# A fused LayerNorm and MLP kernel: another order of loads, statistics and transposes in its opening

## Chip, cores and metric

The kernel runs on one core of a Trainium2 chip. The metric is the device time of one execution in microseconds (us), taken as the median of several runs. All times inside a trace are us from the first instruction of the execution.

## What is computed

x is 2048 x 1024, w1 is 1024 x 3584, w2 is 3584 x 1024, all bfloat16. Cut to what matters:

```python
y = (x - mean(x)) / sqrt(var(x) + 1e-5)          # over the 1024 columns
h = gelu_tanh(y @ w1 + b1)                       # 2048 x 3584
out = h @ w2 + b2                                # 2048 x 1024
```

## The kernel before

The 2048 rows are 16 tiles of 128 rows, and four tiles are one block of 512 rows. For each block the kernel computes all 28 rows of h (a "row" is 128 of the 3584 columns of h, for the 512 rows of x of the block) and then all output chunks of the block. Both products run over the block: 224 matmuls of 128x512 for the first, 224 for the second. Every engine's program is written out as a list of operations with named events. An engine works through its list strictly in that order; an operation that waits holds up everything behind it on its engine.

For blocks 1 to 3 the normalised x is transposed by VectorE while TensorE is busy with the block ahead. Block 0 has nothing ahead of it, so its opening is written out apart, and the change is in that opening alone:

- **Loads.** SP issues x0a (the left half of tile 0), x2, b1, the four pieces w0 to w3 of w1, x3, w4 and then the rest; ScalarE (ACT) issues x0b (the right half of tile 0), x1a and x1b. (Lists at lines 26 and 27; the issue itself is line 182.) w0 and w1 are the upper and lower half of the contraction for rows 0 and 1 of h, w2 and w3 the same for rows 2 and 3. w4 is for rows 4 to 7.
- **LayerNorm on VectorE (DVE).** For each tile there are two bn_stats over 512 columns (line 253), one bn_aggr (line 260), a power on GpSimd (POOL) that makes the inverse deviation (line 257), and the normalisation (line 264). ln_seq (line 278) fixes the order: first statistics of tile i, then the normalisation of tile i-1, then second statistics of tile i, then the aggregate of tile i. So the normalisation of tile 2 stands behind the first statistics of tile 3.
- **Transposes on TensorE (PE).** pe_T (line 316) transposes a tile in eight 128x128 pieces through the identity (line 327); ACT copies the result out of PSUM in two copies of 512 columns (line 333). b1 is transposed in the same way (line 429) and copied to float32 (line 431).
- **First wave.** Before a whole block is there, PE computes rows 0 to 3 of h one tile at a time, with matmuls of 128x128 (line 354): 32 for each tile t, 16 for the upper half of the contraction and 16 for the lower. The eight transposes of tile t+1 (named T1, T2, T3 below) stand between these halves. After the wave come the 128x512 matmuls of rows 4 to 27.
- **Warm-up.** Ahead of the wave PE works through dummy matmuls (line 419): 26 without a gate, 8 behind the first statistics, 8 behind the aggregate, 6 behind the inverse deviation of tile 0, and 3 more after the transposes of tile 0. Line 21 holds these numbers.

The loop of the wave, and the order of the LayerNorm:

```python
for t in range(TPB):
    for h, (j0, j1) in enumerate(KGROUPS):
        for r in range(R):
            pe_cell(0, r, t, t + 1, ..., dts=range(j0, j1))
        if t + 1 < TPB and h == 0:
            pe_T(t + 1)
...
for h in range(2):
    seq.append(op_stats(i, h))
    if h == 0 and prev is not None:
        seq += ops_norm(prev)
seq.append(op_aggr(i))
```

A planner at the end (lines 481 to 496) orders the later work of DVE from estimated times; T_PE_START at line 29 is one of its constants.

Of the kernel before, what the change touches and what calls it, by code (L numbers as in the profile page):

```python
# [5 lines left out]
ACT = mybir.ActivationFunctionType  # L6
ALU = mybir.AluOpType
BF16 = mybir.dt.bfloat16
F32 = mybir.dt.float32
# [10 lines left out]
TAIL_PIECES = 4  # L20
WARM_A = ((26, None), (8, "st0_0"), (8, "mv0"), (6, "rstd0"))
N_WARM_B = 3
W1_CHUNK_COLS = (256, 256, 512, 512, 1024, 1024)
W1_KSPLIT_CHUNKS = 2
N_W2_CHUNKS = 4
SP_FIRST_LOADS = ("x0a", "x2", "b1", "w0", "w1", "w2", "w3", "x3", "w4")
ACT_FIRST_LOADS = ("x0b", "x1a", "x1b")

T_PE_START = 8.5
T_DVE_START = 13.0  # L30
# [54 lines left out]
def bass_standalone__mixer_channel_mlp__prompt_kernel(  # L85
# [20 lines left out]
    assert HC <= 512 and DT * P * 2 <= 2048 and FT >= 4 and FT <= P  # L106
    R = max(1, min(R_WAVE, FT - 2, NB1 - 1))
    nkg = max(1, min(K_GROUPS, DT))
    KGROUPS = [(h * DT // nkg, (h + 1) * DT // nkg) for h in range(nkg)]
    assert NB1 + NB2 + 1 <= 8  # L110

# [30 lines left out]
    with ExitStack() as es:  # L142
# [14 lines left out]
        nhalf = sb("nhalf", [P, NT], F32)  # L157
        st_sb = sb("st_sb", [P, NT, 15], F32)
        mv_sb = sb("mv_sb", [P, NT, 2], F32)
# [4 lines left out]
        ps_2 = ps("ps_2", [P, NB2, 512], F32)  # L164
        ps_1b = ps_1[:, :, :].bitcast(BF16)
        ps_2b = ps_2[:, :, :].bitcast(BF16)
# [38 lines left out]
        def issue(item):  # L205
            if item[0] == "x" and item[-1] in "ab":
                i, h = int(item[1:-1]), "ab".index(item[-1])
                dma(x_sb[:, i, h * HC:(h + 1) * HC], xf[i * P:(i + 1) * P, h * HC:(h + 1) * HC], f"x{i}_{h}",
                    P * HC * 2)
                x_ev[i] = (f"x{i}_0", f"x{i}_1")  # L210
            elif item == "b1":
                dma(b1r_sb[:, :], b1.rearrange("(t p) -> t p", p=P), "b1", F * 2)
            elif item[0] == "x":
                load_x_tile(int(item[1:]))
            elif item[0] == "w" and int(item[1:]) < len(w1_chunks):
                load_w1(int(item[1:]))
# [7 lines left out]
        for i in range(TPB):  # L224
            if i not in x_ev:
                load_x_tile(i)
            else:
                for h, evn in enumerate(x_ev[i]):
                    if evn not in est:
                        issue(f"x{i}" + "ab"[h])  # L230
        if "b1" not in est:
# [16 lines left out]
        pool.op(lambda e: e.memset(nhalf[:, :], -0.5), sig="nhalf")  # L248
        pool.op(lambda e: e.memset(st_sb[:, :, 12:14], 0.0))
        pool.op(lambda e: e.memset(st_sb[:, :, 14:15], LN_EPS * D), sig="eps")  # L250

        def op_stats(i, h):
            return (lambda e, i=i, h=h: e.bn_stats(st_sb[:, i, 6 * h:6 * (h + 1)], x_sb[:, i, h * HC:(h + 1) * HC]),  # L253
                    [x_ev[i][h]], f"st{i}_{h}", 0.65)

        def op_aggr(i):
            pool.op(lambda e, i=i: e.tensor_tensor(out=rstd_sb[:, i:i + 1], in0=mv_sb[:, i, 1:2],  # L257
                                                   in1=nhalf[:, i:i + 1], op=ALU.pow),
                    waits=[f"mv{i}", "nhalf"], sig=f"rstd{i}")
            return (lambda e, i=i: e.bn_aggr(mv_sb[:, i, :], st_sb[:, i, :]),  # L260
                    [f"st{i}_0", f"st{i}_1", "eps"], f"mv{i}", 0.33)

# [8 lines left out]
        def ops_norm(i):  # L271
            if i == 0:
                y_ev[i] = [f"y{i}_{h}" for h in range(2)]
                return [op_norm(i, h * HC, (h + 1) * HC, f"y{i}_{h}") for h in range(2)]
            y_ev[i] = [f"y{i}"] * 2
            return [op_norm(i, 0, D, f"y{i}")]

        def ln_seq(tiles):
            seq = []
            prev = None  # L280
            for i in tiles:
                for h in range(2):
                    seq.append(op_stats(i, h))
                    if h == 0 and prev is not None:
                        seq += ops_norm(prev)
                seq.append(op_aggr(i))
                prev = i
            seq += ops_norm(prev)
            return seq
# [4 lines left out]
        def ops_T(i):  # L294
            blk, t = divmod(i, TPB)
            waits = list(y_ev[i])
            if blk - 2 in mm1_done:
# [15 lines left out]
        pe_t = [T_PE_START]  # L313
        last_te = [None]

        def pe_T(i):
            blk, t = divmod(i, TPB)
            evs = []
            for h, (j0, j1) in enumerate(KGROUPS):
                own = i == 0 and h == 1  # L320
                bank = ps_2b[:, 0, :] if own else ps_t[:, 0, :]
                o0 = j0 if own else 0
                waits = [y_ev[i][h], "ident"]
                if h == 0 and last_te[0] is not None:
                    waits.append(last_te[0])
                for j in range(j0, j1):
                    pe.op(lambda e, i=i, j=j, bank=bank, o0=o0: e.transpose(  # L327
                        out=bank[:, (j - o0) * P:(j - o0 + 1) * P], in_=x_sb[:, i, j * P:(j + 1) * P],
                        identity=ident[:, :]),
                        waits=waits if j == j0 else (), sig=(f"tp{i}_{h}" if j == j1 - 1 else None))  # L330
                src = bank[:, (j0 - o0) * P:(j1 - o0) * P].rearrange("p (j s) -> p j s", j=j1 - j0)
                dst = yT_sb[:, blk % 2, j0:j1, t * P:(t + 1) * P]
                act.op(lambda e, dst=dst, src=src: e.copy(out=dst, in_=src),  # L333
                       waits=[f"tp{i}_{h}" if i == 0 else f"tp{i}_{len(KGROUPS) - 1}"], sig=f"te{i}_{h}")
                evs += [f"te{i}_{h}"] * (j1 - j0)
            yT_ev[i] = evs
            last_te[0] = evs[-1]

        unit_n = [0]
        unit_gelu = []  # L340

        def new_unit():
            u = unit_n[0]
            unit_n[0] += 1
            return u % NB1, ([unit_gelu[u - NB1]] if u >= NB1 else ["b1c"])

        def pe_cell(b, r, t0, t1, bank, waits, sig, dts=None):
# [3 lines left out]
            for k, dt in enumerate(dts):  # L351
                w = (waits if k == 0 else []) + [f"w1c{w1_chunk_of(r, dt)}"]
                w += [yT_ev[b * TPB + t][dt] for t in range(t0, t1)]
                pe.op(lambda e, b=b, r=r, dt=dt, n0=n0, n1=n1, bank=bank: e.matmul(  # L354
                    ps_1[:, bank, n0:n1], lhsT=w1_sb[:, dt, r * P:(r + 1) * P], rhs=yT_sb[:, b % 2, dt, n0:n1],
                    start=(dt == 0), stop=(dt == DT - 1)),
# [5 lines left out]
        def act_gelu(r, t0, t1, bank, wait_ev, sig):  # L362
            n0, n1 = t0 * P, t1 * P
            act.op(lambda e, r=r, n0=n0, n1=n1, bank=bank: e.activation(  # L364
                out=hT_sb[:, r, n0:n1], in_=ps_1[:, bank, n0:n1], func=ACT.Gelu_apprx_tanh,
                bias=b1_sb[:, r:r + 1], scale=1.0),
                waits=[wait_ev, "b1c"], sig=sig)
            unit_gelu.append(sig)

# [16 lines left out]
        def out_chunk(b, st, c0, c1, region, prev_store):  # L386
# [7 lines left out]
            if g >= NB2:  # L394
                waits.append(grp_oe[g - NB2])
            for ft in range(FT):
                pe.op(lambda e, st=st, ft=ft, c0=c0, c1=c1, bank=bank: e.matmul(  # L397
# [19 lines left out]
        def warm(n, gate=None):  # L417
            for _ in range(n):
                pe.op(lambda e: e.matmul(ps_2[:, NB2 - 1, 0:P], lhsT=ones[:, :], rhs=ones[:, :],  # L419
                                         start=True, stop=True), waits=["ones"] + ([gate] if gate else []))  # L420
# [4 lines left out]
        for o in ln_seq(list(range(TPB))):  # L425
            dve_put(o)

        pe_T(0)
        pe.op(lambda e: e.transpose(out=ps_1b[:, NB1 - 1, 0:FT], in_=b1r_sb[:, :], identity=ident[0:FT, 0:FT]),
              waits=["ident", "b1"], sig="b1t")  # L430
        act.op(lambda e: e.copy(out=b1_sb[:, :], in_=ps_1b[:, NB1 - 1, 0:FT]), waits=["b1t"], sig="b1c")  # L431
        warm(N_WARM_B)
        wave = [new_unit() for _ in range(R)]
        for t in range(TPB):
            lastt = (t == TPB - 1)
            for h, (j0, j1) in enumerate(KGROUPS):
                for r in range(R):
                    sig = f"m1_0_{r}" if lastt else f"m1_0_{r}_w{t}"
                    pe_cell(0, r, t, t + 1, wave[r][0], wave[r][1] if (t == 0 and h == 0) else [], sig,
                            dts=range(j0, j1))  # L440
                    if lastt and j1 == DT:
                        act_gelu(r, 0, TPB, wave[r][0], sig, f"g_0_{r}")
                        hT_row[(0, r)] = f"g_0_{r}"
                if t + 1 < TPB and h == 0:
                    pe_T(t + 1)
                    pe_t[0] += DT * 0.056

# [92 lines left out]
```

## Time and profile before

| What | us |
|---|---|
| median of 3 runs | 399.91 |
| lowest and highest of them | 399.84, 399.95 |
| span of the profiled execution, first to last instruction | 398.3 |
| what the median has beyond that span | 1.6 |
| PE busy in the span | 394.9 |
| DVE busy | 137.3 |
| ACT busy | 82.3 |
| first real matmul of the wave starts at | 7.69 |
| last real matmul ends about | 396.5 |

No separate time of the profiled execution is given besides its span; with the 1.6 us around it, it stands at the median. The profile names each group by its source line, engine, operation and tile. "PEld" is the weight load that goes ahead of a matmul. A bracket in a timeline row tells how long the engine had been idle before the row, and what ended the idleness.

### The profile page before, as it was taken

To read this page: it belongs to the slowest core of one execution; us is meant where nothing else is said; L and a number is where in the kernel's file an instruction comes from. 1 tells how busy PE (TensorE), PEld (TensorE's weight loads), DVE (VectorE), ACT (ScalarE), POOL (GpSimd) and SP (SyncE) were. 2 spreads that over 40 slices of the span, in tenths; PEclk is the share of its full clock that TensorE was granted. 3 is DMA by queue.
4 is the path that set the end of the run, shared out by engine and by line. 5 is a ranking of instruction groups with operands and counts; after the bars stand their busy time and mean duration, and the time that the engine had idled before them with its cause. 6 is when DMAs were issued, how large, how long until landed. Compare 5 with 4: busy or idle time off the path is not lost.

```text
span 398.3 us, 4699 instructions
## 1 busy us (share of the span) xinstructions
PE 394.9 (99%) x2056; PEld 189.4 (48%) x2056; DVE 137.3 (34%) x292; ACT 82.3 (21%) x122; POOL 9.7 (2%) x25
## 2 busy tenths in 40 slices
PE   8999999999999999999999999999999999999998
PEld 7744444444444444444444444444444444444447
DVE  5207999899892004988100000001100000001011
ACT  3544430000044332000024334100003344400000
POOL 2002000200010000000000000000000000000000
DMA  8999930000000000000000000000000000000001
GB/s 255 369 387 386 385 146 15 26 13 29 26 1 2 0 0 2 26 15 26 27 15 0 0 2 0 1 27 26 13 28 13 2 0 0 2 13 26 15 26 28
DMA packets 17614, 23.64 MB, mean 59 GB/s; under 512 B 1466, under 2 KB 10042, under 8 KB 17594
## 3 DMA queue, kind: packets, MB, share of 16 engines
q1 hardware_dynamic: 17162, 22.95, 16.6%
q10 hardware_dynamic: 432, 0.39, 0.3%
q8 instruction: 16, 0.26, 0.3%
q14 instruction: 4, 0.03, 0.0%
HBM read 19.14 MB, written 4.19 MB: 59 GB/s over the span
## 4 chain that ended last, share of the span: by engine, by line
PE 99%; ACT 0%; issue 0%; DVE 0%; POOL 0%; POOLq 0%
PE ps L354 49%; PE ps L397 49%; PE ps L419 1%; PE ps_t L327 0%; ACT yT_sb L333 0%; DVE o_sb L408 0%; POOL ones L244 0%; ACT b_sb L431 0%; POOLq L525 0%
## 5 line engine op out<-in xcount | busy, mean ns | idle before, releaser
L354 PE MATMUL ps<-yT_sb,w_sb 128*128 128x512 bf16 (+1 forms) x992 | 194.8, 358 | 0.5 <-ACT b_sb L431 0.5
L397 PE MATMUL ps<-w_sb,hT_sb 128*128 128x512 bf16 (+1 forms) x980 | 194.2, 361 | 0.0
L354 PEld LDWEIGHTS ps<-yT_sb,w_sb 128*128 128x128 bf16 x992 | 91.7, 98 | 102.4 <-ACT b_sb L431 0.7
L397 PEld LDWEIGHTS ps<-w_sb,hT_sb 128*128 128x128 bf16 x980 | 91.3, 98 | 102.6
L364 ACT ACTIVATE hT_sb<-ps,b_sb 128x512 bf16<-128x512 f32 x112 | 76.7, 688 | 257.2 <-PE ps L354 257.2
L305 DVE STREAM_TRANSPOSE yT_sb<-x_sb 32x256 bf16<-32x256 bf16 x192 | 83.7, 436 | 35.0 <-PE ps L354 32.1
L408 DVE TENSOR_TENSOR o_sb<-ps,b_sb 128x512 bf16<-128x512 f32 (+1 forms) x35 | 22.6, 645 | 197.9 <-PE ps L397 197.8
L253 DVE BATCH_NORM_STATS2 st_sb<-x_sb 128x6 f32<-128x512 bf16 x32 | 21.1, 671 | 21.4 <-DMA x_sb<-in_x_dram 21.2
L257 POOL TENSOR_TENSOR rstd_sb<-mv_sb,nhalf 128x1 f32<-128x1 f32 x16 | 8.8, 551 | 111.5 <-DVE mv_sb L260 111.5
L264 DVE TENSOR_SCALAR x_sb<-x_sb,mv_sb,rstd_sb 128x1024 bf16<-128x1024 bf16 (+1 forms) x17 | 8.9, 528 | 3.7 <-POOL rstd_sb L257 2.7
L419 PE MATMUL ps<-ones 128*128 128x128 bf16 x51 | 5.4, 290 | 1.0 <-POOL ones L244 1.0
L419 PEld LDWEIGHTS ps<-ones 128*128 128x128 bf16 x51 | 4.6, 135 | 1.5 <-POOL ones L244 1.0
L333 ACT COPY yT_sb<-ps_t 128x512 bf16<-128x512 bf16 x7 | 3.8, 589 | 7.0 <-PE ps_t L327 7.0
L260 DVE BATCH_NORM_AGGREGATE mv_sb<-st_sb 128x2 f32<-128x15 f32 x16 | 3.6, 222 | 1.5
L327 PE MATMUL ps_t<-ident,x_sb 128*128 128x128 bf16 x28 | 2.2, 220 | 0.0
L422 ACT ACT_TABLE_LOAD x1 | 1.3, 1283 | 2.2 <-issue 2.2
L327 PEld LDWEIGHTS ps_t<-ident,x_sb 128*128 128x128 bf16 x28 | 1.7, 98 | 0.1
L333 ACT COPY yT_sb<-ps 128x512 bf16<-128x512 bf16 x1 | 0.6, 591 | 0.0
L327 PE MATMUL ps<-ident,x_sb 128*128 128x128 bf16 x4 | 0.4, 222 | 0.0
L245 POOL TENSOR_SCALAR_AFFINE_SELECT ident<-ones 128x128 bf16<-128x128 bf16 x1 | 0.3, 294 | 0.1
L327 PEld LDWEIGHTS ps<-ident,x_sb 128*128 128x128 bf16 x4 | 0.2, 98 | 0.1
L244 POOL MEMSET ones<- 128x128 bf16 x1 | 0.2, 205 | 0.3 <-POOLq L525 0.3
(10 smaller groups left out, 1.2 us busy)
## 6 DMA issues: line engine op xcount, KB each, us to landing
w_sb<-in_w_dram SPq DMA_DIRECT2D x4, 1792.0 KB, 18.5
w_sb<-in_w_dram SPq DMA_DIRECT2D x2, 2048.0 KB, 16.7
out_dram<-o_sb SPq DMA_DIRECT2D x31, 128.0 KB, 1.7
x_sb<-in_x_dram SPq DMA_DIRECT2D x3, 1024.0 KB, 14.2
w_sb<-in_w_dram SPq DMA_DIRECT2D x2, 1024.0 KB, 9.2
w_sb<-in_w_dram SPq DMA_DIRECT2D x4, 256.0 KB, 4.7
x_sb<-in_x_dram SPq DMA_DIRECT2D x2, 256.0 KB, 4.4
x_sb<-in_x_dram ACTq DMA_DIRECT2D x3, 128.0 KB, 3.7
```

The lines of the kernel that those rows point to most:

```text
L253: return (lambda e, i=i, h=h: e.bn_stats(st_sb[:, i, 6 * h:6 * (h + 1)], x_sb[:, i, h * HC:(h + 1) * HC]), [x_ev[i][h]], f"st{i}_{h}", 0.65)
L257: pool.op(lambda e, i=i: e.tensor_tensor(out=rstd_sb[:, i:i + 1], in0=mv_sb[:, i, 1:2], in1=nhalf[:, i:i + 1], op=ALU.pow), waits=[f"mv{i} ...
L260: return (lambda e, i=i: e.bn_aggr(mv_sb[:, i, :], st_sb[:, i, :]), [f"st{i}_0", f"st{i}_1", "eps"], f"mv{i}", 0.33)
L264: return (lambda e, i=i, c0=c0, c1=c1: e.tensor_scalar(out=x_sb[:, i, c0:c1], in0=x_sb[:, i, c0:c1], scalar1=mv_sb[:, i, 0:1], scalar2=rst ...
L305: res.append((lambda e, src=src, dst=dst: e.transpose(out=dst, in_=src), waits, (f"tr{i}" if lastop else None), 0.47))
L327: pe.op(lambda e, i=i, j=j, bank=bank, o0=o0: e.transpose(out=bank[:, (j - o0) * P:(j - o0 + 1) * P], in_=x_sb[:, i, j * P:(j + 1) * P], i ...
L333: act.op(lambda e, dst=dst, src=src: e.copy(out=dst, in_=src), waits=[f"tp{i}_{h}" if i == 0 else f"tp{i}_{len(KGROUPS) - 1}"], sig=f"te{i ...
L354: pe.op(lambda e, b=b, r=r, dt=dt, n0=n0, n1=n1, bank=bank: e.matmul(ps_1[:, bank, n0:n1], lhsT=w1_sb[:, dt, r * P:(r + 1) * P], rhs=yT_sb ...
L364: act.op(lambda e, r=r, n0=n0, n1=n1, bank=bank: e.activation(out=hT_sb[:, r, n0:n1], in_=ps_1[:, bank, n0:n1], func=ACT.Gelu_apprx_tanh, ...
L397: pe.op(lambda e, st=st, ft=ft, c0=c0, c1=c1, bank=bank: e.matmul(ps_2[:, bank, 0:c1 - c0], lhsT=hT_sb[:, ft, st * P:(st + 1) * P], rhs=w2 ...
L408: crit.append((est[sig], (lambda e, ob=ob, c0=c0, c1=c1, bank=bank: e.tensor_tensor(out=o_sb[:, ob, c0:c1], in0=ps_2[:, bank, 0:c1 - c0], ...
L419: pe.op(lambda e: e.matmul(ps_2[:, NB2 - 1, 0:P], lhsT=ones[:, :], rhs=ones[:, :], start=True, stop=True), waits=["ones"] + ([gate] if gat ...
```

## The change

The opening of block 0 is arranged anew; the rest of the kernel is as it was.

- **Loads.** Tile 0 comes in four column quarters of 256 columns. SP issues x0a, x0c, x1a, x2, w0 to w3, x3, w4; ACT issues x0b, x0d, x1b, b1.
- **Statistics.** Tile 0 has four bn_stats of 256 columns, and bn_aggr reads 27 values instead of 15. Each tile has its own statistics tensor, so POOL clears them with 32 small memsets instead of 2.
- **Normalisation.** Tile 0 in pieces of 256 and 768 columns, tile 1 in two of 512, tiles 2 and 3 whole as before.
- **Transposes.** Tile 0 in groups of 2, 3 and 3, each with its own PSUM bank and its own copy on ACT; tiles 1 to 3 in two groups of 4, each with its own bank.
- **Order on PE.** For tile 0 rows 0 and 1 are done with both halves of the contraction before rows 2 and 3, piece by piece of the contraction. T1, T2 and T3 stand 8, 16 and 12 matmuls ahead of the end of the part before them (16 in all three before). b1 is transposed behind the matmuls of tile 0, in the bank of the transposes, and the first matmuls wait for b1 no more.
- **Warm-up.** 24 without a gate, 8 behind the first statistics, 8 behind the third, 6 behind the aggregate, 4 behind the inverse deviation, and 4 after the first group of transposes.
- **PSUM.** The first seven accumulation units use the five banks of the first product and the two of the second in turn; then the five go round as before.

```diff
-WARM_A = ((26, None), (8, "st0_0"), (8, "mv0"), (6, "rstd0"))
-N_WARM_B = 3
+WARM_A = ((24, None), (8, "st0_0"), (8, "st0_2"), (6, "mv0"), (4, "rstd0"))
+N_WARM_B = 4
+T_AHEAD = {1: 8, 2: 16, 3: 12}
+NORM_0 = (0, 2, 8)
+GROUPS_0 = (0, 2, 5, 8)
+NORM_1 = {1: (0, 4, 8)}
+GROUPS_1 = (0, 4, 8)
-SP_FIRST_LOADS = ("x0a", "x2", "b1", "w0", "w1", "w2", "w3", "x3", "w4")
-ACT_FIRST_LOADS = ("x0b", "x1a", "x1b")
-
-T_PE_START = 8.5
+X0_PARTS = 4
+SP_FIRST_LOADS = ("x0a", "x0c", "x1a", "x2", "w0", "w1", "w2", "w3", "x3", "w4")
+ACT_FIRST_LOADS = ("x0b", "x0d", "x1b", "b1")
+
+T_PE_START = 6.9
...
-        pool.op(lambda e: e.memset(st_sb[:, :, 12:14], 0.0))
-        pool.op(lambda e: e.memset(st_sb[:, :, 14:15], LN_EPS * D), sig="eps")
+        for i in range(NT):
+            n = 6 * parts(i)
+            pool.op(lambda e, i=i, n=n: e.memset(st_sb[i][:, n:n + 2], 0.0))
+            pool.op(lambda e, i=i, n=n: e.memset(st_sb[i][:, n + 2:n + 3], LN_EPS * D), sig=f"eps{i}")
...
-            return u % NB1, ([unit_gelu[u - NB1]] if u >= NB1 else ["b1c"])
+            bank = first_ring[u] if u < len(first_ring) else ("1", (u - len(first_ring)) % NB1)
+            waits = [bank_gelu[bank]] if bank in bank_gelu else []
...
+        def pe_b1():
+            pe.op(lambda e: e.transpose(out=ps_t[:, 0, 0:FT], in_=b1r_sb[:, :], identity=ident[0:FT, 0:FT]),
+                  waits=["ident", "b1", bank_read["t"]], sig="b1t")
+            act.op(lambda e: e.copy(out=b1_sb[:, :], in_=ps_t[:, 0, 0:FT]), waits=["b1t"], sig="b1c")
+            bank_read["t"] = "b1c"
+
+        pe_T(0, GROUPS_0, 0)
         warm(N_WARM_B)
+        for k in range(1, len(GROUPS_0) - 1):
+            pe_T(0, GROUPS_0, k)
...
+            if t == 0:
+                part = []
+                for r0 in range(0, R, 2):
+                    for j0, j1 in KGROUPS:
+                        part += cells(0, range(r0, min(R, r0 + 2)), j0, j1, True)
+            else:
+                part = []
+                for j0, j1 in KGROUPS:
+                    part += cells(t, range(R), j0, j1, False)
+            if t + 1 < TPB:
+                at = len(part) - T_AHEAD[t + 1]
+                part[at:at] = [("T", t + 1)]
+                if t == 0:
+                    part.append(("b1",))
```

## The prediction

> **What bounds the kernel now.** I read the page first. PE is busy 99% of the span, and the chain that ended last lies on PE for 99%. So the end moves only if PE's continuous work starts earlier or gets a hole. Then I read the chain in order of time:
>
> ```profile
> 1.04 5.04 PE ps L419 x48
> 6.09 0.36 PE ps_t L327 x4
> ...
> 6.47 1.07 ACT yT_sb L333 x2
> 7.54 0.10 ACT b_sb L431
> ...
> 7.69 1.07 PE ps L354 x16
> 8.75 0.45 PE ps_t L327 x8
> 9.20 1.79 PE ps L354 x32
> 10.99 0.47 PE ps_t L327 x8
> 11.46 1.79 PE ps L354 x32
> 13.24 0.45 PE ps_t L327 x8
> 13.69 44.12 PE ps L354 x240
> ```
>
> Columns: start, us, what. From 7.69 on PE never pauses. One 128x128 matmul takes 1.79 / 32 = 0.056 us, one transpose the same (0.45 / 8). From 13.69 on nothing in the change touches PE's work. The question is when the wave can get through, that is, what each piece of it waits for besides PE. The timeline of DVE in the middle of the wave:
>
> ```profile
> 8.37 0.69 DVE L253 BATCH_NORM_STATS2 st_sb<-x_sb 128x6 f32<-128x512 bf16 x1
> 9.15 0.22 DVE L260 BATCH_NORM_AGGREGATE mv_sb<-st_sb 128x2 f32<-128x15 f32 x1
> 9.63 0.69 DVE L253 BATCH_NORM_STATS2 st_sb<-x_sb 128x6 f32<-128x512 bf16 x1 [0.26 <-DMA x_sb<-in_x_dram]
> 10.24 0.53 DVE L264 TENSOR_SCALAR x_sb<-x_sb,mv_sb,rstd_sb 128x1024 bf16<-128x1024 bf16 x1
> ```
>
> The row at 9.63 is the first statistics of tile 3: DVE idles 0.26 until x3 has landed. Behind it stands the normalisation of tile 2, which ends at 10.24 + 0.53 = 10.78. T2's first weight load is the row at 10.83:
>
> ```profile
> 8.54 0.49 PEld L327 LDWEIGHTS ps_t<-ident,x_sb 128*128 128x128 bf16 x8
> ...
> 10.83 0.45 PEld L327 LDWEIGHTS ps_t<-ident,x_sb 128*128 128x128 bf16 x8
> ```
>
> PE arrives there at about the same moment, so the table of waits shows no wait. But there is hardly any reserve: **T2 cannot start before x3 has landed plus about 1.22** (0.61 from the start of the statistics to that of the normalisation, 0.53, 0.05 to PE, 0.02 to wake DVE). Last, the DMA view around two issues, at 3.1 to 3.3 and at 4.2 to 4.4:
>
> ```profile
> w_sb<-in_w_dram SPq DMA_DIRECT2D x2, 256.0 KB, 4.7
> ```
> ```profile
> x_sb<-in_x_dram SPq DMA_DIRECT2D x1, 256.0 KB, 5.3
> ```
>
> The second, issued at 4.28, is x3: it lands 5.3 later, at 9.6, after a queue of everything ahead. The first holds two pieces of w1. The later one, issued at 3.19, is w2, which lands 4.9 after its issue, at 8.0; w3 (issued at 3.74, 5.1) lands at 8.9. From 4 to 9.6 the stretches show 300 to 375 GB/s and a DMA share about 1.0 or above: the queue is full.
>
> **The change, part by part.**
>
> *Loads up to x3.* Ahead of and with x3 stand the same bytes as before: x0 to x3, 1 MB, and w0 to w3, 1 MB, and b1. Only the packets of x0 shrink, from 1 KB to 512 B. Rows: from 5 to 6 there are 665 packets and 0.33 MB (512 B each) at 330 GB/s; from 7 to 8, 544 packets, 298 GB/s; from 9.62 to 11, 478 packets, 0.49 MB (1 KB each), 355 GB/s. x0's 0.262 MB take 0.74 at the last rate and 0.79 to 0.88 at the first two: +0.05 to +0.14, I take +0.1. Upwards: the opening from 1.75 to 3 runs at 131 to 316 GB/s; at 209, its second lowest stretch, x0 takes 1.25 against 0.74, +0.5. Downwards: 0.29 MB have moved by 3.0; at 330 GB/s from 1.8 it would be 0.40, so quarters that fill the opening better could save at most 0.11 / 0.33 = 0.3. SP issues eight DMAs ahead of x3 instead of seven, at about 0.5 each; x3 is issued at 4.8 instead of 4.28 and still waits some 4.9 in the queue, so this costs nothing; without that cover it would cost 0.5. b1 leaves SP's queue for the end of ACT's; the table load on ACT behind it starts 0.45 later (2.18 to 2.6) and ends by 3.9, long before ACT's first copy. So w2 lands at 8.14, w3 at 9.0, x3 at 9.7.
>
> The Trainium skill, "DMA: Bandwidth & Descriptors", section "Bandwidth", speaks against the quarters: its table has 138 GB/s for a DMA of 64 KB, and calls smaller ones descriptor-dominated. An estimate from that rate for x0 is 1.9 us, which would put the time at about 401.1. The trace's rate for DMAs queued behind each other decides here.
>
> *Statistics of tile 0.* DVE starts when x0a has landed: 3.23 before; a quarter brings half the bytes, so between 2.7 (0.13 MB less on both queues at about 250 GB/s) and 3.23. Two statistics of 512 take 1.29 (the row at 3.23: x2); four of 256 take between 1.29 (cost by columns) and 2.5 (cost by instruction: four pitches of 0.61). The normalisations have 0.53 for 1024 columns and about 0.40 for 512, so there is a fixed part; I take 1.45. The aggregate starts between 4.2 and 5.8 and likeliest at 4.4, against 4.61. DVE's next work shifts by as much, and x1a should be there (it is now ahead of x2).
>
> The Trainium skill, "VectorE: DVE Perf Modes", section "The TRN2 errata — SBUF-src ops pay a fixed extra latency per instruction", tells one to keep tiles at 512 elements or more, since each instruction pays the latency again; its 58 cycles at 0.96 GHz give, as an estimate, 2 x 0.06 more for four instead of two, which is 0.1 and moves nothing at T2.
>
> *POOL.* 32 memsets instead of 2. Rows: the two start 0.04 and 0.06 after the operation before them, and last 0.13. At 0.05 apart they end at 1.34 + 1.6 = 2.9, hidden under the wait for x0; at 0.13 one after the other they end at 5.5, and the inverse deviation would come up to 0.9 late. I take the pitch.
>
> *Warm-up and first matmul.* 40 dummies stand ahead of the aggregate's gate; the 26 ungated loads take 2.69 from 1.04, 0.104 each, so 40 end at about 5.3, and ten at 0.056 end at 5.9. Normalisation of 256 columns is ready at about 5.6, so PE gets to the first transposes at 5.9. Two transposes, four dummies, six transposes: 6.6. The copy on ACT (0.59 for 512 columns, 0.4 for 256 by the same kind of scaling) ends at 6.6. The first real matmul is at about **6.65 instead of 7.69**, and it no longer waits for b1.
>
> *What is late next.* Rows 0 and 1 need w0 and w1 (landed 6.3 and 7.2), then the copies; they are through at about 7.8. Rows 2 and 3 need **w2, at 8.14**: PE stands 0.35 there. 8 matmuls to 8.64; T1, 8 transposes, to 9.09 (tile 1 normalised by about 8.3); 8 matmuls to 9.53; the transpose of b1 waits for the first copy of T1 (copy 9.06 to 9.65), 9.76 with it; 16 matmuls of tile 1 to 10.65. Queued behind b1's transpose is all of PE, but this wait is in front of the next one. **T2 needs tile 2 normalised: x3 at 9.71 + 1.22 = 10.93.** PE stands again, 0.28. Behind T2 both kernels have the same work: 16 matmuls of tile 1, tiles 2 and 3, T3. T3 moves 4 matmuls back, which gives its normalisation (ready at 12.92 + 0.1, PE there at 13.4) more room. The copies of T3 have 12 matmuls, 0.67, in front of their first reader and need 0.17 + 0.22 + 0.04 + 0.59 + 0.05 = 1.07 from the start of T3; with its own 0.45 PE gives 1.12. It just fits.
>
> *Later blocks.* PE has no idle time there; the planner's new constant moves a few DVE operations, the transposes for blocks 1 to 3 are long ready. Nothing.
>
> **Sum.** T2 goes from 10.83 to 10.93: span 398.3 + 0.1, with 1.6 around it **400.0**. The gain of 1.0 at the first matmul is eaten by w2 (down to about 0.2 at T2's place) and by x3 (gone).
>
> **Rivals.** What a measurement of this kernel can tell from no change is about 0.2%, 0.8 us.
>
> 1. *The opening moves as a whole* (1.0 earlier: 398.9). It needs w2 and x3 to land 0.8 or more sooner. Against it: a full queue and the same bytes. 0.04.
> 2. *Part of it arrives* : x3 lands as before or up to 0.3 sooner, T2 between 10.5 and 10.83 (PE's side and DVE's free time at about 9.2 allow no earlier): 399.55 to 399.85. 0.15.
> 3. *DVE or POOL late* : statistics by instruction or memsets end to end, +0.7 to +0.9 at the aggregate. DVE's 0.26 of idleness ahead of x3's statistics, and 0.1 for the later x3, are the cover; what exceeds them is paid: 400.25 to 400.6. Also x3 late by 0.5: 400.4. 0.11.
> 4. *PE falls back to the slow pitch* in the wave (the slower side). Place: the stalls at 6.9, 7.8, 9.6 and 10.65, together about 1.1 between 6.65 and 10.93. Price: the slow stretch before lasted 4.3 (1.04 to 5.3) at 0.104 against 0.056; again 4.3 at that pitch loses 2.0: 402.0. It decides from a pause longer than the 0.54 that PE has before 7.69 now, after which the pitch stays 0.056. No single stall of mine is longer. 0.05.
>
> My forecast, T2 held by x3, 399.85 to 400.25: 0.65. The range goes from rival 2's lower end to 400.6: rivals 1 and 4 stay out. Faster by over 0.2%: 0.04; within: 0.90; slower: 0.06.
>
> **What would show it.** Right: first matmul of the wave at 6.5 to 6.8; a wait of PE for w2; x3's statistics again right after a DMA wait, at 9.6 to 9.9; T2 at 10.8 to 11.1 after PE idleness. Wrong: T2 before 10.5 (x3 is not the limit), 0.1 us pitches after 7, or aggregates after 4.9.

## The result

| Kernel | runs | median us | lowest to highest |
|---|---|---|---|
| before | 22 | 399.90 | 399.64 to 400.62 |
| changed | 22 | 400.54 | 400.00 to 401.33 |

The ratio is 1.0013, with a 95% interval of 1.0007 to 1.0019: 0.5 us slower, clear of noise but within the 0.2% that I called no change. (The two medians stand 0.64 apart.) The time lies in the range, 0.54 above the forecast of 400.0, but only 0.06 below the range's upper end: it is in the band of rival 3, and not in the 399.85 to 400.25 to which I gave 0.65. The profiled execution took 400.68, with a span of 399.3, 1.0 above the span before. That difference is on the large side: 398.3 belongs to a short execution of the kernel before, whose spans beside the experiments have medians of 398.5 to 398.7, and the changed kernel's 22 spans have one of 399.05. One execution among the experiments, the profiled one of e1, took 462.69 where its ten neighbours took 399.86 to 401.09, and is left out of e1's ratio.

### The profile page after: what moved, and what is told of

Read it like the earlier page. It is cut to its first block, busy times and chain, and to the rows that moved or that the text cites. A ratio compares the mean times of both kernels' runs of the same rounds, so it can differ in the third digit from the quotient of the medians.

```text
span 399.3 us, 4691 instructions
## 1 busy us (share of the span) xinstructions
PE 393.3 (99%) x2024; PEld 189.4 (47%) x2059; DVE 138.0 (35%) x295; ACT 82.4 (21%) x123; POOL 10.6 (3%) x55
## 4 chain that ended last, share of the span: by engine, by line
PE 97%; DMA 1%; SPq 1%; issue 1%; DVE 0%
PE ps L420 48%; PE ps L375 48%; DMA w_sb<-in_w_dram 1%; SPq L189 1%; PE ps_t L342 0%; PE ps L342 0%; DVE o_sb L431 0%; PE ps_t L452 0%
## 5 line engine op out<-in xcount | busy, mean ns | idle before, releaser
L264 DVE BATCH_NORM_STATS2 st_sb<-x_sb 128x6 f32<-128x512 bf16 (+1 forms) x34 | 21.2, 639 | 21.5 <-DMA x_sb<-in_x_dram 21.5
L276 DVE TENSOR_SCALAR x_sb<-x_sb,mv_sb,rstd_sb 128x1024 bf16<-128x1024 bf16 (+3 forms) x18 | 9.1, 513 | 3.8 <-POOL rstd_sb L269 2.6
L272 DVE BATCH_NORM_AGGREGATE mv_sb<-st_sb 128x2 f32<-128x15 f32 (+1 forms) x16 | 3.6, 226 | 0.6
L348 ACT COPY yT_sb<-ps_t 128x512 bf16<-128x512 bf16 (+1 forms) x4 | 2.1, 532 | 7.0 <-PE ps_t L342 7.0
L348 ACT COPY yT_sb<-ps 128x512 bf16<-128x512 bf16 (+1 forms) x5 | 2.6, 548 | 0.1
L342 PE MATMUL ps<-ident,x_sb 128*128 128x128 bf16 x18 | 1.7, 220 | 0.0
L342 PEld LDWEIGHTS ps<-ident,x_sb 128*128 128x128 bf16 x18 | 1.1, 98 | 0.1
L259 POOL MEMSET st_sb<- 128x2 f32 x16 | 1.1, 99 | 0.0
L260 POOL MEMSET st_sb<- 128x1 f32 x16 | 1.1, 98 | 0.0
```

The costliest lines, as they stand in the source:

```text
L264: return (lambda e, i=i, h=h, pw=pw: e.bn_stats(st_sb[i][:, 6 * h:6 * (h + 1)], x_sb[:, i, h * pw:(h + 1) * pw]), [x_ev[i][h if len(x_ev[i ...
L276: return (lambda e, i=i, c0=c0, c1=c1: e.tensor_scalar(out=x_sb[:, i, c0:c1], in0=x_sb[:, i, c0:c1], scalar1=mv_sb[:, i, 0:1], scalar2=rst ...
L342: pe.op(lambda e, i=i, j=j, o=(j - j0) * P, bap=bap: e.transpose(out=bap[:, o:o + P], in_=x_sb[:, i, j * P:(j + 1) * P], identity=ident[:, ...
```

## The profile after

First the page's share of the chain by line. Loads stand in it now, which were not there before:

```profile
PE ps L420 48%; PE ps L375 48%; DMA w_sb<-in_w_dram 1%; SPq L189 1%; PE ps_t L342 0%; PE ps L342 0%; DVE o_sb L431 0%; PE ps_t L452 0%
```

The chain in order of time (start, us, what) runs through SP's issues, then through the load of w2, and through PE from there:

```profile
3.66 5.33 DMA w_sb<-in_w_dram
8.99 0.05 issue
9.04 0.62 PE ps L375 x8
...
10.82 1.00 PE ps L375 x16
11.82 0.01 issue
11.82 0.38 PE ps_t L342 x4
```

w2 lands at 8.99 instead of 8.0, and T2's first transpose stands at 11.82 instead of 10.84. The timeline of DVE (tiles 2 and 3 before the change stand in the prediction; here are tiles 0 and 1 before, and then the timeline after):

```profile
4.97 0.69 DVE L253 BATCH_NORM_STATS2 st_sb<-x_sb 128x6 f32<-128x512 bf16 x1
5.59 0.72 DVE L264 TENSOR_SCALAR x_sb<-x_sb,mv_sb,rstd_sb 128x512 bf16<-128x512 bf16 x2
```
```profile
4.57 0.28 DVE L272 BATCH_NORM_AGGREGATE mv_sb<-st_sb 128x2 f32<-128x27 f32 x1
5.63 0.69 DVE L264 BATCH_NORM_STATS2 st_sb<-x_sb 128x6 f32<-128x512 bf16 x1 [0.78 <-DMA x_sb<-in_x_dram]
6.24 0.72 DVE L276 TENSOR_SCALAR x_sb<-x_sb,mv_sb,rstd_sb 128x256 bf16<-128x256 bf16 x2
...
10.54 0.69 DVE L264 BATCH_NORM_STATS2 st_sb<-x_sb 128x6 f32<-128x512 bf16 x1 [0.46 <-DMA x_sb<-in_x_dram]
11.15 0.53 DVE L276 TENSOR_SCALAR x_sb<-x_sb,mv_sb,rstd_sb 128x1024 bf16<-128x1024 bf16 x1
```

The reader is to see two waits for loads. At 5.63 the first statistics of tile 1 wait for x1a (landed 5.61), and the normalisation of tile 0 stands behind them, although its inverse deviation has been ready since 5.49. At 10.54 the statistics of tile 3 wait for x3 (landed 10.51, not 9.61), and the normalisation of tile 2 stands behind them and ends at 11.68. PE loses most of its early start by the first, and waits for w2 at 9.04:

```profile
6.63 0.28 PE L342 MATMUL ps_t<-ident,x_sb 128*128 128x128 bf16 x2 [0.68 <-DVE x_sb L276]
...
7.46 1.35 PE L375 MATMUL ps<-yT_sb,w_sb 128*128 128x128 bf16 x16
9.04 0.62 PE L375 MATMUL ps<-yT_sb,w_sb 128*128 128x128 bf16 x8 [0.22 <-DMA w_sb<-in_w_dram]
```

Which of the two late loads holds T2? The chain names w2, but the weight loads ahead of T2 tell more:

```profile
10.62 0.09 PEld L452 LDWEIGHTS ps_t<-ident,b1r_sb 28*128 28x128 bf16 x1 [0.24 <-issue]
10.75 0.90 PEld L375 LDWEIGHTS ps<-yT_sb,w_sb 128*128 128x128 bf16 x16
11.79 0.24 PEld L342 LDWEIGHTS ps_t<-ident,x_sb 128*128 128x128 bf16 x4 [0.15 <-issue]
```

By its own work since w2, PE was ready for T2 at 11.65 (10.75 + 0.90). T2 began 0.14 later, 0.11 after tile 2 was normalised. So x3 holds T2, but only just: by this reckoning the late w2 alone would still have put T2 some 0.8 behind its old place.

Both kernels do the same work from T2 on, and indeed span minus T2 is 387.5 in both (399.3 - 11.82, 398.3 - 10.84). So the 1.0 of the span is all in T2's start. The question is why the loads are late.

## Experiments

Each experiment has a label, e1 to e12. Its time is compared with that of the kernel before, measured beside it; landings and starts are those of its one profiled execution. Theory A was that T2 hangs on the landing of x3 and w2, and that the quarters make these late. Rivals: B, the new order of the loads; C, the new order on PE; D, the 32 memsets on GpSimd; E, w2 alone.

**e1: halves in the changed kernel.** Only the quarters are undone (loads and statistics of tile 0, and the event behind which eight dummies stand):

```diff
...
-X0_PARTS = 4
-SP_FIRST_LOADS = ("x0a", "x0c", "x1a", "x2", "w0", "w1", "w2", "w3", "x3", "w4")
-ACT_FIRST_LOADS = ("x0b", "x0d", "x1b", "b1")
+X0_PARTS = 2
+SP_FIRST_LOADS = ("x0a", "x1a", "x2", "w0", "w1", "w2", "w3", "x3", "w4")
+ACT_FIRST_LOADS = ("x0b", "x1b", "b1")
```

> The changed kernel with tile 0 loaded in halves and with statistics of halves, so that only the quarters are undone; order of loads, groups of transposes and order on PE as changed. Theory A (the quarters delay every load behind them, and w2 and x3 set the wave): w2 and x3 land as before, 8.0 to 8.2 and 9.6 to 9.8, T2 at about 10.8, time 399.8 to 400.0. Rival B (the new order of the loads, x1a on SP ahead of x2 and b1 on ACT, causes the delay): x3 still lands at 10.3 or later, time 400.4 to 400.7.

400.55 (400.50 without the 462.69) against 399.78, ratio 1.0018 (1.0009 to 1.0027); w2 at 8.69, x3 at 10.17, T2 at 11.73. The trace is that of the 462.69, and its matmuls are slow already behind T2 (36 in 2.43, where the changed kernel takes 2.17), so it counts little. The time is what rival B expects. Undoing the quarters alone has won nothing back: this run speaks against A, and I come back to it.

**e2: old loads in the changed kernel.** All loads as before, the rest as changed:

```diff
...
-X0_PARTS = 4
-SP_FIRST_LOADS = ("x0a", "x0c", "x1a", "x2", "w0", "w1", "w2", "w3", "x3", "w4")
-ACT_FIRST_LOADS = ("x0b", "x0d", "x1b", "b1")
+X0_PARTS = 2
+SP_FIRST_LOADS = ("x0a", "x2", "b1", "w0", "w1", "w2", "w3", "x3", "w4")
+ACT_FIRST_LOADS = ("x0b", "x1a", "x1b")
```

> The changed kernel with all loads as before (halves, x2 and b1 on SP, x1 on ACT), so that only the work on the engines is changed. Theory A and rival B (the loads are at fault): w2 at 8.0, x3 at 9.6, T2 at 10.8, time 399.7 to 400.0. Rival C (the new order on PE, the groups and their waits are at fault, whatever the loads do): 400.4 to 400.7, with T2 at 11.3 or later.

400.04 against 399.78, ratio 1.0007 (0.9998 to 1.0016); w2 at 8.34, x3 at 9.89, T2 at 11.20. The time is 0.4 below the least that rival C expects, so the new order on PE does not cost the 0.6, though the interval leaves room for a part of it. The loads are somewhat late in this execution too, which A did not expect. And the new order gains nothing, although the first real matmul is at 6.96 instead of 7.69: the gain is gone at T2, as forecast. e1 and e2 differ in the order of the loads alone, and in time by 0.46.

**e3: quarter loads alone in the kernel before.**

```diff
-SP_FIRST_LOADS = ("x0a", "x2", "b1", "w0", "w1", "w2", "w3", "x3", "w4")
-ACT_FIRST_LOADS = ("x0b", "x1a", "x1b")
+SP_FIRST_LOADS = ("x0a", "x0c", "x2", "b1", "w0", "w1", "w2", "w3", "x3", "w4")
+ACT_FIRST_LOADS = ("x0b", "x0d", "x1a", "x1b")
...
```

> The kernel before with nothing changed but tile 0 in four loads (each statistics of 512 columns waits for two of them), in the queues that its halves had. Theory A: w2 at 8.5 to 9.0, x3 at 10.1 to 10.5, T2 at 11.3 to 11.8, time 400.3 to 400.9. Rivals B and C: x3 within 0.2 of 9.6, time 399.8 to 400.1.

400.58, ratio 1.0027 (1.0012 to 1.0042). Two of its twelve runs, at 402.4 and 403.7, had a mean granted clock of 0.996 and 0.992; the other ten have a median of 400.55 and stand 0.16% above the kernel before in the mean. In time A is right, but not in its mechanism. In the profiled execution, one of the shortest at 400.18, w2 and x3 land earlier than A expects (8.32, 9.83). T2 at 11.40 is late because x0's third and fourth quarter land at 4.18 and 4.36 and the second statistics wait for them:

```profile
4.46 0.69 DVE L255 BATCH_NORM_STATS2 st_sb<-x_sb 128x6 f32<-128x512 bf16 x1 [0.67 <-DMA x_sb<-in_x_dram]
```

**e4: new order of the loads alone in the kernel before.**

```diff
-SP_FIRST_LOADS = ("x0a", "x2", "b1", "w0", "w1", "w2", "w3", "x3", "w4")
-ACT_FIRST_LOADS = ("x0b", "x1a", "x1b")
+SP_FIRST_LOADS = ("x0a", "x1a", "x2", "w0", "w1", "w2", "w3", "x3", "w4")
+ACT_FIRST_LOADS = ("x0b", "x1b", "b1")
```

> The kernel before with nothing changed but the order of the loads: SP x0a, x1a, x2, w0 and so on, ACT x0b, x1b, b1, in halves. Theory A: x3 within 0.2 of 9.6, time 399.8 to 400.1. Rival B: x3 at 10.2 or later, time 400.4 or more.

399.93, ratio 1.0004 (0.9995 to 1.0012), x3 at 9.58. As A expects; in the kernel before, the order of x1, x2 and b1 by itself is harmless.

**e5: four memsets in the changed kernel.** One statistics tensor for all tiles, 27 values for each:

```diff
-        for i in range(NT):
-            n = 6 * parts(i)
-            pool.op(lambda e, i=i, n=n: e.memset(st_sb[i][:, n:n + 2], 0.0))
...
+        for i0, i1 in ((0, 1), (1, NT)):
+            n = 6 * parts(i0)
+            pool.op(lambda e, i0=i0, i1=i1, n=n: e.memset(st_all[:, i0:i1, n:n + 2], 0.0))
...
```

> The changed kernel with four memsets of the statistics on GpSimd instead of 32. Theory A (the time is that of T2, which hangs on x3's and w2's landing; GpSimd plays no part): 400.3 to 400.7, as the changed kernel. Rival D (the memsets at 1.3 to 2.5 disturb the first loads): x1a by 4.7, x3 by 9.8, time 399.8 to 400.1.

400.10 against 399.86, ratio 1.0003 (0.9995 to 1.0012): below what A expects and at the upper edge of what D expects. x1a lands at 4.43, as D expects, x3 at 10.07, which D does not. e12 repeats it.

**e6: 32 memsets alone in the kernel before.**

```diff
-        st_sb = sb("st_sb", [P, NT, 15], F32)
+        st_sb = [sb(f"st_sb{i}", [P, 15], F32) for i in range(NT)]
...
+        for i in range(NT):
+            pool.op(lambda e, i=i: e.memset(st_sb[i][:, 12:14], 0.0))
+            pool.op(lambda e, i=i: e.memset(st_sb[i][:, 14:15], LN_EPS * D), sig=f"eps{i}")
...
```

> The kernel before with 32 memsets on GpSimd (a statistics tensor for each tile) and nothing else changed. Theory A: 399.7 to 400.0, as before. Rival D: 400.2 or more, x3 at 9.9 or later.

399.93, ratio 1.0002 (0.9993 to 1.0011), x3 at 9.56. In the kernel before, the memsets cost nothing, against rival D.

**e7: normalisations first in the changed kernel.**

```diff
                 for h in range(parts(i)):
+                    if h == 0 and i in (1, 3):
+                        seq += ops_norm(prev)
                     seq.append(op_stats(i, h))
-                    if h == 0 and prev is not None:
+                    if h == 0 and prev is not None and i not in (1, 3):
                         seq += ops_norm(prev)
```

> The changed kernel with the normalisation of tile 0 ahead of the first statistics of tile 1 on VectorE, and that of tile 2 ahead of the first statistics of tile 3, so that neither waits for a load of the next tile. Theory A: the first transposes start at 5.9 to 6.1 instead of 6.6, tile 2 is normalised before x3 lands, and T2 is then held by w2 and PE's own work: T2 0.15 to 0.4 earlier relative to x3's landing (less than x3 + 1.1), time 400.1 to 400.4. Rival E (w2 alone holds the wave, the order on VectorE does not count): T2 not earlier than w2 + 2.7 and time 400.4 to 400.7.

400.08 against 399.86, ratio 1.0005 (0.9996 to 1.0013). The times lie between 399.96 and 400.19, the narrowest of all kernels (the changed one: 400.00 to 401.33, and 399.96 to 400.71 in e9), and in the median below what either side expected by a little. First transposes at 5.94, first real matmul at 6.77. But T2 is at 11.13, x3 (9.80) + 1.33: another wait has taken the place of x3, on DVE:

```profile
9.55 0.22 DVE L272 BATCH_NORM_AGGREGATE mv_sb<-st_sb 128x2 f32<-128x15 f32 x1
10.44 0.55 DVE L276 TENSOR_SCALAR x_sb<-x_sb,mv_sb,rstd_sb 128x1024 bf16<-128x1024 bf16 x1 [0.66 <-POOL rstd_sb L269]
```

GpSimd's power, 0.55, was hidden under the statistics of the next tile and now stands open. So the order with the statistics first has its price (it takes on the jitter of a load) and its use. By time A is right, by T2's place A is wrong (x3 + 1.33 is not less than x3 + 1.1) and E's condition is met (w2 at 8.23, T2 2.9 later). The trace decides for neither: PE has done its work ahead of T2 at 10.89 (16 matmuls of 0.056 from 9.99), and tile 2 is normalised at 10.99, held by DVE's own chain.

**e8: wide w1 pieces, meant to beat both.** Beside halves of x0, four memsets, the normalisations first, and all four rows of h in each half of tile 0's contraction:

```diff
-W1_CHUNK_COLS = (256, 256, 512, 512, 1024, 1024)
-W1_KSPLIT_CHUNKS = 2
+W1_CHUNK_COLS = (512, 512, 512, 1024, 1024)
+W1_KSPLIT_CHUNKS = 1
...
+SP_FIRST_LOADS = ("x0a", "x1a", "w0", "x2", "w1", "x3", "w2")
+ACT_FIRST_LOADS = ("x0b", "x1b", "b1")
```

> A version meant to be faster than both: x0 in halves, SP x0a, x1a, upper half of w1 for rows 0 to 3 (rows of 1 KB in place of 512 B), x2, lower half, x3; ACT x0b, x1b, b1; all four rows of h in each half of the contraction of tile 0; four memsets; the normalisations of tiles 0 and 2 first. Theory A: the w1 pieces need fewer packets, x3 lands by 9.3, T2 at 10.3 to 10.7, time 399.4 to 399.7. If packets do not matter: x3 at 9.6 or later, T2 at 10.7 or later, 399.8 or more.

A clear miss: 400.88, ratio 1.0030 (1.0017 to 1.0043). The first piece of w1 lands at 8.08, and T2 is at 12.89. In the traces each load of x and w1 reports its landing 16 times, part by part. The first part of this piece reports at 5.78, the last at 8.08; some part is 2.3 behind the first, and the later loads in the queue keep about the same gap (x3: 8.71 and 10.91).

**e9: the changed kernel again, unaltered**, beside the three that follow.

> The changed kernel once more, unaltered, as the yardstick for the three beside it on the same chip. Theory A: its profiled span is 398.3 + (T2 - 10.83) to within 0.1, with T2 at its x3's landing + 1.2 to 1.35 or at its w2's + 2.5 to 2.9, whichever is later; time 400.1 to 400.7.

400.36 against 400.01, ratio 1.0009 (1.0000 to 1.0017). w2 at 9.03, x3 at 10.55, T2 at 11.86, and 398.3 + 1.02 = 399.3 is its span. As A expects: T2 is x3 + 1.31. The slow landing is no accident of one execution.

**e10: x3 behind w4 in the kernel before**, a dose of lateness for x3 alone:

```diff
-SP_FIRST_LOADS = ("x0a", "x2", "b1", "w0", "w1", "w2", "w3", "x3", "w4")
+SP_FIRST_LOADS = ("x0a", "x2", "b1", "w0", "w1", "w2", "w3", "w4", "x3")
```

> The kernel before with one pair of loads exchanged: x3 behind w4 (1 MB) instead of ahead of it. Theory A (T2 is x3's landing + 1.22): x3 lands 2.8 to 3.2 later, T2 as much, time 402.6 to 403.1. Rival (PE's order or w2 holds T2, x3's place is covered): under 400.5.

404.11 (402.73 to 404.37; four runs). x3 lands at 12.56, 2.95 later, and T2 starts at 13.78, 2.94 later: x3 + 1.22, the rule of the prediction to the hundredth. That alone makes a span of 401.2, and the one run with an undiminished clock has 401.5 (402.73 in time, as A expects). The three others have a mean granted clock of 0.996 and are beyond what A expects; in the profiled one PE fell back to its slow pitch at the end of the wait. PE's timeline, and then the stretches (A:B, length; busy time of PE, PEld, DVE, ACT and POOL with their instructions; granted clock; DMA share, which is the time of the packets that start in the stretch as a share of 16 DMA engines; GB/s of these packets):

```profile
13.78 1.02 PE L327 MATMUL ps_t<-ident,x_sb 128*128 128x128 bf16 x8 [2.05 <-DVE x_sb L264]
14.59 3.22 PE L354 MATMUL ps<-yT_sb,w_sb 128*128 128x128 bf16 x32
```
```profile
15.00:16.00 1.00, 1.00 (x13) 1.00 (x11) 0.55 (x1) 0.90 (x2) 0.28 (x1) 0.50 1.06 385
16.00:17.00 1.00, 1.00 (x12) 1.00 (x11) 0.00 (x0) 0.00 (x0) 0.00 (x0) 0.50 1.07 391
17.00:18.00 1.00, 1.00 (x19) 1.00 (x17) 0.00 (x0) 0.00 (x0) 0.00 (x0) 0.87 1.05 385
```

32 matmuls take 3.2 instead of 1.8, at a granted clock of 0.50, from 13.8 to about 17. It costs 402.9 - 401.2, some 1.6 in unrounded figures.

**e11: interleaved order.** PE gets other work in front of w2 and x3; beside that, four memsets, and the normalisation of tile 2 first:

```diff
+        order += cells(0, first, 0, 4, True) + cells(0, first, 4, DT, True)
+        order += [("T", 1)]
+        order += cells(0, second, 0, 4, True)
+        order += cells(1, first, 0, 4, False) + cells(1, first, 4, DT, False)
+        order += [("b1",)]
+        order += cells(0, second, 4, DT, True)
+        order += [("T", 2)]
+        order += cells(1, second, 0, 4, False) + cells(1, second, 4, DT, False)
...
```

> The changed kernel with four memsets, with the normalisation of tile 2 ahead of the first statistics of tile 3, and with another order on PE: rows 0 and 1 of tile 0, T1, upper half of rows 2 and 3 of tile 0, rows 0 and 1 of tile 1, b1, lower half of rows 2 and 3 of tile 0, T2, rows 2 and 3 of tile 1, and then as before. Neither w2 nor x3 stands in front of idle time of PE. Theory A: T2 at 10.4 to 10.8 after the same work as otherwise plus nothing, time 399.4 to 399.8, below the kernel before. If the loads hold the wave in another way: 400.0 or more.

399.90 against 400.01 of before and 400.36 of the changed kernel beside it; ratio to before 1.0000 (0.9991 to 1.0008). That is 0.46 below the changed kernel, about what that had lost (the four memsets and DVE's order may have a part in it), but no gain over before: A's 399.4 to 399.8, with T2 at 10.4 to 10.8, is missed. T2 is at 11.23 and no longer hangs on x3 (10.50), but the first matmuls wait for w0 (7.14) and w1 (8.04), which are late as well:

```profile
7.19 0.62 PE L377 MATMUL ps<-yT_sb,w_sb 128*128 128x128 bf16 x8 [0.48 <-DMA w_sb<-in_w_dram]
8.09 0.62 PE L377 MATMUL ps<-yT_sb,w_sb 128*128 128x128 bf16 x8 [0.28 <-DMA w_sb<-in_w_dram]
```

The new order covers w2 and x3, and lays bare the two loads ahead of them.

**e12: four memsets again**, beside the changed kernel.

> The run with four memsets once more, beside the changed kernel on the same chip. Theory A (GpSimd plays no part): within 0.25 of the changed kernel beside it. Rival D (the 32 memsets disturb the loads): 0.3 to 0.6 below it, and the changed kernel's spread of times the wider one.

400.14 (399.76 to 401.30), ratio to before 1.0009 (1.0000 to 1.0017), 0.22 below the changed kernel and with the wider spread. Its profile is the latest of all with these loads: x1a 5.97, x3 10.91, T2 12.22, span 399.7. The ratio to before is that of the changed kernel in e9, 1.0009, and 0.22 is within A's 0.25, so with e6 nothing is left that speaks for rival D but the time of e5.

**What the traces have in common.** The stretch from 2.75 to 3.5, when x0 has mostly arrived, tells the kernels apart. The kernel before, the changed kernel, its repetition (e9), and the new order with halves (e4):

```profile
2.75:3.50 0.75, 0.75 (x10) 0.75 (x9) 0.27 (x1) 0.72 (x1) 0.00 (x0) 1.00 1.08 258
```
```profile
2.75:3.50 0.75, 0.75 (x10) 0.75 (x8) 0.37 (x2) 0.61 (x1) 0.00 (x0) 1.00 1.04 116
```
```profile
2.75:3.50 0.75, 0.75 (x10) 0.75 (x8) 0.41 (x2) 0.61 (x1) 0.00 (x0) 1.00 1.29 140
```
```profile
2.75:3.50 0.75, 0.75 (x10) 0.75 (x9) 0.00 (x0) 0.75 (x1) 0.00 (x0) 1.00 1.10 351
```

The last column is GB/s. Over all traces:

| Loads of tile 0 | GB/s from 1.75 to 2.75 | GB/s from 2.75 to 3.5 | x3 lands at |
|---|---|---|---|
| halves (before, e1, e2, e4, e6, e8, e10) | 154 to 235 | 258 to 374 | 9.56 to 10.17 in the first five |
| quarters, x2 next on SP (e3) | 175 | 268 | 9.83 |
| quarters, x1a next on SP (changed, e5, e7, e9, e11, e12) | 158 to 221 | 93 to 196 | 9.80 to 10.91 |

In the third row the loads have a hole. It is not that the DMA engines have nothing to do: their share stays at 0.81 to 1.29, because some packets take long. The changed kernel's stretch in two parts:

```profile
2.75:3.00 0.25, 0.25 (x5) 0.25 (x4) 0.00 (x0) 0.11 (x1) 0.00 (x0) 1.00 2.20 269
3.00:3.50 0.50, 0.50 (x8) 0.50 (x5) 0.37 (x2) 0.50 (x1) 0.00 (x0) 1.00 0.46 40
```

The packets that start before 3.0 run far beyond it, and behind them little starts. Five packets of 1 KB that start between 2.94 and 3.14 take 0.63 to 0.92 us each; from 3.5 to 3.75 the longest takes 0.05. x1a, issued at 1.69, lands at 5.61, whereas x1a issued at 1.22 in e4 has landed whole at 4.14. At 350 GB/s in place of 116 the stretch would have brought 0.18 MB more, which is 0.5 us at that rate, and from 4.5 to 9 the changed kernel's loads (324 GB/s) hardly make it up against before (318). The mean of x3's landing is 9.76 in the five traces with halves and the old place of x3, and 10.39 in the six of the third row: 0.6 later.

A landing is the last of a load's 16 reports, so it can be late in two ways: the whole load comes late, or one part lags behind. The mean of x3's 16 reports tells them apart:

| x3 | mean of its 16 reports | last report (landing) |
|---|---|---|
| before | 9.29 | 9.61 |
| changed | 9.76 | 10.51 |
| e1 (halves in the changed kernel) | 9.39 | 10.17 |
| five traces with halves, mean | 9.28 | 9.76 |
| six traces of the third row, mean | 9.74 | 10.39 |

Of the 0.63 between the last two rows, 0.46 is the whole load, about the size of the hole, and 0.17 the last part's lag. Of the 0.90 in the changed kernel's own trace, the lag is nearly half, 0.43. In e1 nearly all is lag.

**What stays open.** Why x1a brings so little before 3.4 (how many loads were ahead, the time of issue, the size of packets go together here), and why some packets take so long, and why in some executions one part of a load falls behind by up to 2. And e1: no hole in that stretch (357 GB/s), yet as slow as the changed kernel. Its loads in the kernel before (e4) are harmless, the work of the engines with the old loads (e2) nearly so; the two together are not, and its only trace is that of the 462.69. So a late x3 and w2 are shown to be what T2 pays for, but what makes them late is not shown. The quarters cost about as much by themselves in the kernel before (e3), by a late x0 in its one trace, and there is a hole in every trace where x1a follows them; taking them out of the changed kernel does not end its loss (e1).

## Why the prediction was right, and where it was off

The time was forecast by the right mechanism, and with one term far too small. That it stayed in the range was in part luck, as point 4 says. Of the four signs that I named for being right, one came as stated, PE's wait for w2; the first matmul (7.46), x3's statistics (10.54) and T2 (11.82) were all 0.6 to 0.7 later than the windows given.

1. **T2 sets the end; right.** Span minus T2's first transpose lies between 387.4 and 387.5 in before, changed, e2 to e6, e8, e9, e11 and e12, with T2 between 10.84 and 12.89 (387.6 in e7).
2. **"T2 cannot start before x3 has landed plus about 1.22"; right as a bound.** T2 is at x3 + 1.22 in e10, the dose, and at x3 + 1.31 in the changed kernel, e2, e5, e9 and e12, so the new order adds 0.09. In the kernel before, x3 and PE's own work tied: T2 is there at the first real matmul + 3.15. In e3, e4 and e6, which keep PE's old order, T2 is at the first matmul + 3.13 to 3.14 and x3 had landed 1.4 to 1.6 before it. There it was PE's start that set T2, and not x3.
3. **The early start is eaten by w2 and x3; right.** e2 starts 0.7 earlier and ends no earlier.
4. **"Loads up to x3 ... I take +0.1"; this is the term that was mis-sized.** Measured: +0.9 for x3 and +0.95 for w2 in the profiled execution, +0.6 for x3 in the mean of the traces. I counted the bytes and the packets' rate in a full queue. The first stretch is indeed no slower with quarters (158 to 221 GB/s against 154 to 235), but I took the queue to run at its full rate behind it. The hole from 2.75 to 3.5 was in none of my bounds' reasons, and neither was a lagging part. The upper bound, +0.5, was near the mean all the same, by another working (a slow first stretch), and that is luck.
5. **"x1a should be there"; wrong.** It landed at 5.61, 0.78 after DVE wanted it. So the first transposes were at 6.63 instead of 5.9, and the first real matmul at 7.46 instead of 6.65. e7, where the normalisation does not wait for x1a, has 5.94 and 6.77. For the end this miss was covered: PE stood waiting for w2 at 9.04 anyway. (In e5, e7 and e11, with the same loads, x1a landed between 4.43 and 4.67, so it is not always late.)
6. **Statistics, memsets, dummies; right.** Four statistics take 1.40 (1.45 forecast), the memsets start 0.035 apart and end at 2.5, PE is through its dummies at 5.95. The estimate of 0.1 from the Trainium skill ("VectorE: DVE Perf Modes", the section on the TRN2 errata) agrees with the trace: 1.40 for four against 1.29 for two.
7. **The wait at b1's transpose; right in kind.** The weight loads stand idle 0.24 there (the row at 10.62), where I had 0.1 to 0.2, in front of the next wait.
8. **Rival 1 fell, rival 3's second half came closest** (x3 late by 0.5: 400.4, within a rival that I gave 0.11). Rival 4, the slow pitch, is real, but not in the changed kernel: its granted clock is 1.000. In e10 it took a pause of 2.05 and cost 1.6, where I had priced 2.0.
9. The Trainium skill's rate of 138 GB/s for a load of 64 KB ("DMA: Bandwidth & Descriptors", section "Bandwidth") would have given 401.1. It spoke against the quarters, and my row of a full queue was the wrong one to set against it. But the measured 400.54 is well below 401.1, and the trace does not agree with the rate: all queues together moved 158 to 221 GB/s while x0 came, and x0 was not what was late (its quarters land by 3.65 in the changed kernel, its halves by 3.38 to 3.70 in the traces with halves).

The miss in time is 0.54 of 400.54. Point 4 accounts for it in size: x3 later by 0.6 in the mean of the traces, the median time later by 0.64, where I had 0.1 for both. Why x3 and w2 come that much later stays open.

## What to carry to other kernels

When a chain of loads feeds a pipeline, find the last load that something waits for, and write each landing down; an earlier start is worth nothing past the next landing. Cutting a first load into smaller ones got the first piece sooner here (the first statistics start at 2.85 to 3.13 instead of 3.23 to 3.54), but the loads behind it landed later in the mean, so look at what happens to the load that follows, and do not only count the bytes. An operation that waits for a load and has other work queued behind it passes each hiccup of that load on; with the ready work ahead of it the times of e7 spread over 0.2, where the changed kernel's spread over 0.75 and 1.3, at the price of laying bare a wait that had been covered. (e8 and e11 put normalisations first too and spread over 2.0 and 1.5; there PE waits for weights.) And a single profiled execution is not the median: the one before the change was shorter than the median, and in the one after it a lagging part made half of x3's lateness.

## What the runs showed of the hardware

- One load's 16 parts can report far apart: 0.6 for x3 before, 1.26 in the changed kernel, 2.2 in e8. In the changed kernel the gap is 1.5 at x1a (first report at 4.10, last at 5.61) and is still 1.26 at x3.
- Single packets of 1 KB took 0.63 to 0.92 us at about 3.0 in the changed kernel, and 0.61 to 0.93 in e9. Loads were then moving 40 and 81 GB/s (3.0 to 3.5).
- PE fell back to half clock after 2.05 us of idleness in the profiled run of e10, and stayed there for 3.4 us (0.50 to 0.52 in the rows from 13.8 to 17, and 0.87 in the next); two more of its four runs have the same mean clock of 0.996, the fourth has 1.0. The Trainium skill ("TensorE: Matmul & The Clock Gate", section "Part 1: The HAM clock gate") puts this after an idle window of about 3.4 us; here a shorter pause was enough in that run. The pauses of up to 0.7 in the changed kernel left the granted clock at 1.00.
